# A fused attention and mixture kernel: a buffer for the third raw tile, two clears on VectorE, and a new place for six weight copies

## The chip, the cores and the metric

The kernel runs on one core of a Trainium2 chip. The metric is the device time of one execution in microseconds; of several executions the median is given. Engines: TensorE (PE, with its weight loads as PEld), VectorE (DVE), ScalarE (ACT), GpSimd (POOL) and SyncE (SP), whose queue issues nearly all loads and many of the stores.

## What is computed

Three layers follow one another on 8 batches of 576 tokens. The reference, cut to what matters:

```python
def attn(q, k, v, w_phi):                  # 8 heads of 64, d_feat 128
    def phi(x):
        proj = x @ w_phi
        proj = proj - max(abs(proj))       # over the features
        return concat([exp(proj), exp(-proj)])
    kv = einsum('bhsf,bhsd->bhfd', phi(k), v)
    z = sum(phi(k), axis=2)
    return (phi(q) @ kv) / (phi(q) @ z + 1e-06)

def moe(x):                                # 4 experts, the best 2 per token
    for e in range(4):
        a = softmax(causal(0.125 * (x @ wq[e]) @ (x @ wk[e]).T))
        out += gate[e] * (a @ (x @ wv[e]) @ wo[e])

def moe2(x):                               # mixes each token with the one before
    k = relu(xk @ w_k); v = (k * k) @ w_v
    return sigmoid(xr @ w_r) * v
```

## The kernel before, in words

The first layer is `favor`. For each batch and each half of the heads (`g` 0 and 1) the keys come as five tiles, `GROUPS`: four of 256 tokens and, third, one of 128. A key tile (`k_unit`) goes through a chain. `load` (line 273) brings the raw tile on SP's queue; `sp` splits it into a high part on ScalarE (`hi`, line 97) and a low part on POOL (`lo`, line 100), so that fp32 products come out of fp32r matmuls; `proj` makes three matmuls per 128 tokens, high by high, high by low, low by high (lines 288 to 290), into a PSUM tile `pj`, of which there are two for batch 0; `norm` reduces the maximum (line 298) and subtracts it (line 300, `pm`) on VectorE; `norm2` makes the two exponentials `ph` on ScalarE (lines 323 and 324); `kvmm` multiplies them with the values `vx`, loaded at line 315, in fp32 (line 343, `kv`). Batch 0 has ten key tiles, called one to ten here. Query tiles take a similar way over `tq` (line 370), `num` (386), `xs` (393) and `xt` (400).

The raw tiles have the tag `raw` with two buffers. The third load can be issued when tile one's high and low part have been made. `skewed` runs these stages as a software pipeline, and `weave` interleaves `favor` with the other streams: `moe1`, `compose` (the output weights times the third layer's, line 117 `fo`), `decodes` (weights that come as 64-bit floats), `load_moe1` and `gates_keys` (`rk`). From this the framework's scheduler makes one fixed order for each engine, by its own estimate of times; each engine then takes its instructions in that order.

Ahead of the weave stand the opening's pieces. The projection weights `wphi` are loaded and split on VectorE (lines 99 and 100). VectorE clears `one`, with which six filler matmuls are made on TensorE (line 138, `busy`). `clear_pads` clears padding on POOL: `k2z` (lines 149, 150), two pieces of `vsp` (152), `at1` (154), `yf` (156). Three steps of `favor` are traced, then the loads of four constants (line 979), then the weave starts. `load_moe1` loads the query, key and value projection weights of the second layer in six pieces (line 164) and splits each, the high part by ScalarE (line 97, `wqh`, `wkh`, `wvh`), the low part by VectorE (line 100, `wql`, `wkl`, `wvl`). Output weights are loaded at line 212 (`wof`) and split on VectorE (`sw`).

Of the kernel before, what the change touches and what calls it, by code (L numbers as in the profile page):

```python
# [6 lines left out]
F32 = mybir.dt.float32  # L7
F32R = mybir.dt.float32r
AF = mybir.ActivationFunctionType
# [4 lines left out]
P = 128  # L14
# [20 lines left out]
def place(fns, at):  # L35
    out = [None] * (at[-1] + 1)
    for f, a in zip(fns, at):
        out[a] = f
    return out
# [37 lines left out]
def fused_kernel(ctx: ExitStack, tc: tile.TileContext, qT, kT, vx, wphi, wq, wk, wvg, wo, mu, w64, ident, cmask, tri, out):  # L77
    nc = tc.nc
# [13 lines left out]
    def eng(c):  # L92
        return {'v': nc.vector, 'p': nc.gpsimd}[c]

    def split(hi, lo, src, eh=None, el=None):
        if eh == 'a':
            nc.scalar.activation(hi, src, AF.Copy)  # L97
        else:
            nc.vector.tensor_copy(hi, src)
        (el or nc.vector).tensor_sub(lo, src, hi.bitcast(F32))  # L100

    def evac(e, o, i):
        if e == 'a':
            nc.scalar.activation(o, i, AF.Copy)
        else:
            nc.vector.tensor_copy(o, i)
    state = {}

    def tg(n):
        return dict(tag=LATE.get(n, TAGS[n]) if 'favored' in state else TAGS[n], bufs=2)  # L110
# [19 lines left out]
    pF = phF.enter_context(tc.tile_pool(name='pF', bufs=1))  # L130
# [16 lines left out]
    def clear_pads():  # L147
        for t in K2Z:
            nc.gpsimd.memset(t[64:P, 0].bitcast(F32), 0.0)
            nc.gpsimd.memset(t[0:64, 1].bitcast(F32), 0.0)  # L150
        for t in VSP:
            nc.gpsimd.memset(t[64:P, 4].bitcast(F32), 0.0)
        for t in AT1:
            nc.gpsimd.memset(t[64:P, 1280:1600].bitcast(F32), 0.0)
        for t in YF:
            nc.gpsimd.memset(t[:, 0:1], 0.0)

    def load_moe1():
        for src, h, l, n in ((wq, wqh, wql, 'p a b c -> p (a b c)'), (wk, wkh, wkl, 'p a b c -> p (a b c)'), (wvg, wvh, wvl, 'p a b -> p (a b)')):
            hf, lf, sf = (h.rearrange(n), l.rearrange(n), src.rearrange(n))  # L160
            w = hf.shape[1] // 2
            for i in range(2):
                s_ = pA.tile([P, S], F32, name='wst1', tag='a', bufs=3)
                nc.sync.dma_start(s_[:, :w], sf[:, i * w:(i + 1) * w])
                split(hf[:, i * w:(i + 1) * w], lf[:, i * w:(i + 1) * w], s_[:, :w], 'a')
                yield 40

    def decode(pool, i, rawkw, sq, cost=1, pool_raw=None):
# [87 lines left out]
    def spans(t, h0):  # L256
        if t < 4:
            return [(0, P, h0, P * t)]
        if t > 4:
            return [(0, P, h0 + 1, P * t - S)]  # L260
        return [(0, 64, h0, 512), (64, P, h0 + 1, 0)]

    def favor(b):
        kvbank = {}

        def proj_stages(src, g, u, dst, first=False):
            tl = GROUPS[u]
            nt = len(tl)
            n = nt * P

            def load():
                t_ = pF.tile([P, 256], F32, name='raw', tag='raw', bufs=2)
                nc.sync.dma_start(t_[:, :n], src[b, g, :, tl[0] * P:tl[0] * P + n])
                dst['raw'] = t_

            def sp():
                hi = pF.tile([P, 256], F32R, name='hi', tag='hi', bufs=2)
                lo = pF.tile([P, 256], F32R, name='lo', tag='lo', bufs=2)
                split(hi[:, :n], lo[:, :n], dst['raw'][:, :n], 'a', eng('p' if b else 'p' if first else 'p'))
                dst['hl'] = (hi, lo)  # L280

            def proj():
                ps = psA.tile([P, 512], F32, name='pj', tag='f' if b else 's', bufs=2)
                hi, lo = dst['hl']
                for i in range(nt):
                    c = slice(i * P, (i + 1) * P)
                    o = ps[:, i * 256:(i + 1) * 256]
                    nc.tensor.matmul(o, hi[:, c], wph, start=True, stop=False)  # L288
                    nc.tensor.matmul(o, hi[:, c], wpl, start=False, stop=False)  # L289
                    nc.tensor.matmul(o, lo[:, c], wph, start=False, stop=True)  # L290
                dst['ps'] = ps
                return nt * 327

            def norm():
                g = 2 * nt
                ps = dst['ps'][:, :g * P].rearrange('p (g f) -> p g f', f=P)
                m = pF.tile([P, 4], F32, name='m', tag='m', bufs=3)
                nc.vector.tensor_reduce(m[:, :g], ps, axis=AX.X, op=OP.max, apply_absolute_value=True)  # L298
                pm = pF.tile([P, 512], F32, name='pm', tag='pm', bufs=3)
                nc.vector.tensor_sub(pm[:, :g * P].rearrange('p (g f) -> p g f', f=P), ps, m[:, :g].unsqueeze(2).to_broadcast([P, g, P]))  # L300
                dst['pm'] = pm
            return (load, sp, proj, norm)
        fk = [0, 2, 4, 5, 7]

        def k_unit(g, u):
            d = {}
            tl = GROUPS[u]
            nt = len(tl)
            load, sp, proj, norm = proj_stages(kT, g, u, d, True)

            def norm3():
                v_ = pF.tile([P, 2, 2, 65], F32, name='vx_', tag='vx', bufs=3)
                t0 = tl[0] + (u > 2)
                nv = 2 if u == 2 else nt
                nc.sync.dma_start(v_[:, :nv], vx[b, g, :, t0:t0 + nv])
                d['v'] = v_
                norm2()

            def norm2():
                norm()  # L320
                n = nt * 256
                kp = pF.tile([P, 2, 512], F32, name='ph', tag='ph', bufs=2)
                nc.scalar.activation(kp[:, 0, :n], d['pm'][:, :n], AF.Exp)
                nc.scalar.activation(kp[:, 1, :n], d['pm'][:, :n], AF.Exp, scale=-1.0)  # L324
                d['kp'] = kp

            def kvmm(sel):
                cost = 0
                for i, t in enumerate(tl):
                    for lo_, hi_, hp, s0 in spans(t, 2 * g):  # L330
                        if len(spans(t, 2 * g)) == 2 and hp != 2 * g + sel:
                            continue
                        new = (hp, b) not in kvbank
                        if new:
                            bank = psK.tile([P, 512], F32, name='kv', tag='kv', bufs=1)
                            kvbank[hp, b] = (bank if b == 0 else bank[:, :260]).rearrange('p (r d) -> p r d', r=4)
                        bank = kvbank[hp, b]
                        end = s0 + (hi_ - lo_) == S
                        for r in range(4):
                            c0 = (2 * i + r // 2) * P  # L340
                            v = d['v'][:, i + (lo_ > 0)]
                            v = v.rearrange('p j d -> p (j d)')[:, 2 * (r // 2):2 * (r // 2) + P] if b == 0 else v[:, r // 2]
                            nc.tensor.matmul(bank[:, r, :], d['kp'][:, r % 2, c0:c0 + P], v, start=new and r == 0, stop=end, skip_group_check=True)  # L343
                            cost += 224
                        if end:
                            kvt = pF.tile([P, 260], F32, name='kvs', tag=f'kvs{b % 2}', bufs=4)
                            if b == 0:
                                k4 = kvt.rearrange('p (r d) -> p r d', r=4)
                                evac('a', k4[:, 0:2], bank[:, 0:2, 0:65])
                                evac('a', k4[:, 2:4], bank[:, 2:4, 63:P])  # L350
                            else:
                                evac('a', kvt, bank.rearrange('p r d -> p (r d)'))
                            kvs[hp, b] = kvt
                return cost
            if nt == 1:
                return place([load, sp, proj, norm3, lambda: kvmm(0), lambda: kvmm(1)], fk + [fk[-1] + 1])
            return place([load, sp, proj, norm3, lambda: kvmm(0)], fk)
# [438 lines left out]
    def moe2():  # L796
# [173 lines left out]
        def all_():  # L970
            yield from first()
            yield from skewed([t for c in range(NC_) for t in chunk(c)])
        return all_()
    clear_pads()
    fs, ms, rk, m2 = (favors(), skewed(moe1()), skewed(gates_keys()), moe2())
    for _ in range(3):
        next(fs)
    for dst, src in ((idn, ident), (cm, cmask), (trs, tri), (mus, mu)):
        nc.sync.dma_start(dst, src)
# [55 lines left out]
```

## Time and profile before

| | |
|---|---|
| median of 3 runs | 1240.56 us (1239.51 to 1241.06) |
| the profiled execution | 1243.16 us |
| its span, first to last instruction | 1241.2 us |
| TensorE busy | 1207.8 us (97%) |
| VectorE busy | 941.5 us (76%) |
| ScalarE busy | 817.8 us (66%) |
| POOL busy | 428.1 us (34%) |
| mean granted clock of TensorE | 0.997 |

The rows come from the one profiled execution, its sums stand against 1243.16 us. Times in rows count from the span's start. A matmul's record includes the time in which it drains, so neighbouring records overlap, and the distance between starts tells the pace. The fp32 matmuls have two records each.

### The profile page before, as it was taken

How to read it: one execution, taken by the hardware profiler on the slowest of the kernel's cores; microseconds unless marked ns; L12 is line 12 of the kernel's file. 1: busy time of each engine (PE TensorE's matmuls, PEld its weight loads, DVE VectorE, ACT ScalarE, POOL GpSimd, SP SyncE). 2: the span in 40 equal slices, each digit the busy share in tenths (PEclk: the TensorE clock that was granted, in tenths of full speed). 3: DMA queues.
4: the chain of work that ended last, by engine and by line, in shares of the span. 5: the costliest groups of instructions: out<-in, count | busy, mean ns of one | idle time of the engine just before them, and what ended most of it. 6: DMA issues, size and time to landing. Idle time of an engine off the chain costs nothing.

```text
span 1241.2 us, 26673 instructions
## 1 busy us (share of the span) xinstructions
PE 1207.8 (97%) x9014; PEld 1168.1 (94%) x9014; DVE 941.5 (76%) x2493; ACT 817.8 (66%) x2008; POOL 428.1 (34%) x630
## 2 busy tenths in 40 slices
PE   8999999999999999999999999989999999999998
PEld 7899989999999999999999999988898899999998
DVE  7875988888977777887888768857757677756866
ACT  6565767667767776775668767577668575456534
POOL 5542666445643333644544533332211100000000
PEclk9999999999999999999999999999999999999999
DMA  7323125313224443454456444675788998899843
GB/s 205 93 85 90 63 84 163 110 54 104 102 91 145 137 152 116 121 168 144 124 157 181 125 139 121 183 232 164 231 277 279 311 354 288 291 309 301 283 146 128
DMA packets 159271, 212.71 MB, mean 171 GB/s; under 512 B 34464, under 2 KB 115232, under 8 KB 159136
## 3 DMA queue, kind: packets, MB, share of 16 engines
q1 hardware_dynamic: 145312, 192.12, 49.7%
q10 hardware_dynamic: 13824, 18.88, 4.2%
q8 instruction: 73, 1.20, 0.4%
q14 instruction: 62, 0.51, 0.1%
HBM read 145.94 MB, written 65.01 MB: 170 GB/s over the span
## 4 chain that ended last, share of the span: by engine, by line
PE 82%; DVE 6%; DMA 5%; ACT 2%; POOL 2%; issue 1%; SPq 0%; ACTq 0%; POOLq 0%; DVEq 0%
PE rk L117 16%; PE vacc L909 13%; PE kv L343 10%; PE num L386 8%; PE qk L117 7%; PE vp L117 4%; PE yp L601 3%; PE at L566 3%; PE pj L288 3%; PE fo L117 2%; PE pj L290 2%; PE pj L289 2%; PE tq L370 2%; PE sc L528 2%; PE sc L529 2%; DMA wt<-wf 1%
## 5 line engine op out<-in xcount | busy, mean ns | idle before, releaser
L559 POOL TENSOR_SCALAR a<-a,sv,gw 128x128 f32<-128x128 f32 (+4 forms) x160 | 107.5, 673 | 226.8 <-DVE sv L553 90.0
L100 POOL TENSOR_TENSOR lo<-raw,hi 128x256 fp32r<-128x256 f32 (+1 forms) x160 | 109.2, 685 | 183.5 <-ACT hi L97 170.2
L386 PE MATMUL num<-kvs,ph 128*128 128x65 f32 (+1 forms) x1280 | 142.0, 262 | 0.2 <-DVE xs L393 0.2
L386 PEld LDWEIGHTS num<-kvs,ph 128*128 128x128 f32 (+1 forms) x1280 | 137.1, 181 | 4.1 <-issue 1.2
L298 DVE TENSOR_REDUCE m<-pj 128x4 f32<-128x512 f32 (+1 forms) x160 | 100.7, 631 | 35.2 <-PE pj L290 33.8
L909 PE MATMUL vacc<-XT,wch 128*128 128x384 f32 x480 | 123.4, 334 | 0.7 <-DVE XT L100 0.7
L548 ACT ACTIVATE a<-sc,sv 128x128 f32<-128x128 f32 (+2 forms) x192 | 98.1, 513 | 16.9 <-DVE sv L543 9.1
L741 DVE TENSOR_TENSOR z<-rk,z 128x384 f32<-128x384 f32 x144 | 79.1, 551 | 39.6 <-PE rk L117 32.8
L300 DVE TENSOR_TENSOR pm<-pj,m 128x512 f32<-128x512 f32 (+1 forms) x160 | 100.2, 629 | 4.6 <-ACT ph L324 2.0
L543 DVE TENSOR_REDUCE sv<-sc 128x1 f32<-128x128 f32 (+2 forms) x192 | 88.5, 468 | 5.1 <-PE sc L529 1.9
L288 PE MATMUL pj<-wph,hi 128*128 128x256 f32 x288 | 90.0, 313 | 2.1 <-DVE pm L300 1.2
L97 ACT ACTIVATE XT<-kx 128x1536 fp32r<-128x1536 f32 x40 | 59.4, 1487 | 47.8 <-PE vacc L909 40.4
L100 DVE TENSOR_TENSOR XT<-kx,XT 128x1536 fp32r<-128x1536 f32 x40 | 70.1, 1753 | 24.6 <-ACT XT L97 24.5
L909 PEld LDWEIGHTS vacc<-XT,wch 128*128 128x128 f32 x480 | 86.8, 188 | 1.1 <-DVE XT L100 1.1
L97 ACT ACTIVATE hi<-raw 128x256 fp32r<-128x256 f32 (+1 forms) x160 | 62.0, 392 | 33.1 <-PE pj L289 8.8
L290 PE MATMUL pj<-wph,lo 128*128 128x256 f32 x288 | 82.5, 287 | 0.4 <-POOL lo L100 0.4
L289 PE MATMUL pj<-wpl,hi 128*128 128x256 f32 x288 | 82.0, 285 | 0.0
L909 PE MATMUL vacc<-XT,wcl 128*128 128x384 f32 x240 | 79.5, 334 | 0.0
L566 PE MATMUL at<-idn,a 128*128 128x128 f32 (+2 forms) x480 | 72.9, 261 | 5.1 <-POOL a L559 5.0
L743 ACT ACTIVATE z<-z 128x384 f32<-128x384 f32 x96 | 50.1, 521 | 33.7 <-DVE z L741 32.5
L583 DVE TENSOR_TENSOR at1l<-at,at1h 128x384 fp32r<-128x384 f32 (+3 forms) x128 | 59.2, 462 | 13.9 <-ACT at1h L582 11.5
L582 ACT ACTIVATE at1h<-at 128x384 fp32r<-128x384 f32 (+3 forms) x128 | 53.4, 418 | 24.3 <-PE at L566 16.9
(531 smaller groups left out, 3692.0 us busy)
## 6 DMA issues: line engine op xcount, KB each, us to landing
wt<-wf SPq DMA_DIRECT2D x216, 256.0 KB, 3.3
kd<-z ACTq DMA_DIRECT2D x96, 192.0 KB, 3.2
kx<-kd SPq DMA_DIRECT2D x21, 768.0 KB, 6.7
yd<-yt SPq DMA_DIRECT2D x16, 864.0 KB, 4.5
kd<-z SPq DMA_DIRECT2D x48, 192.0 KB, 3.8
zs<-kd SPq DMA_DIRECT2D x12, 768.0 KB, 6.9
out_dram<-o SPq DMA_DIRECT2D x24, 384.0 KB, 3.2
raw<-in_kT_dram SPq DMA_DIRECT2D x64, 128.0 KB, 2.4
```

Source lines behind the costliest of these rows:

```text
L97: nc.scalar.activation(hi, src, AF.Copy)
L100: (el or nc.vector).tensor_sub(lo, src, hi.bitcast(F32))
L117: nc.tensor.matmul(ps, a, m, start=first and i == 0, stop=last and i == n - 1)
L288: nc.tensor.matmul(o, hi[:, c], wph, start=True, stop=False)
L289: nc.tensor.matmul(o, hi[:, c], wpl, start=False, stop=False)
L290: nc.tensor.matmul(o, lo[:, c], wph, start=False, stop=True)
L298: nc.vector.tensor_reduce(m[:, :g], ps, axis=AX.X, op=OP.max, apply_absolute_value=True)
L343: nc.tensor.matmul(bank[:, r, :], d['kp'][:, r % 2, c0:c0 + P], v, start=new and r == 0, stop=end, skip_group_check=True)
L386: nc.tensor.matmul(ps[lo_:hi_, i, j, :], d['qp'][:, hf, c0 + lo_:c0 + hi_], kvs[hp, b][:, r * 65:(r + 1) * 65], start=hf == 0, stop=hf == 1)
L559: eng(asc).tensor_scalar(a[:m, :nk], a[:m, :nk], rc[:m], WT[b][:m, i, e:e + 1], op0=OP.mult, op1=OP.mult)
L566: nc.tensor.transpose(ps[:kw, jj * m:jj * m + m], d['a'][:m, jj * P:jj * P + kw], idn[:m, :m])
L909: nc.tensor.matmul(ps, a[:, f, dp], m[:, f], start=j in (0, 1, 5) and n == 0, stop=n == 11, skip_group_check=True)
```

## The change

It has three parts. The third raw tile of batch 0 takes its buffer from the tag `xs`, which has the same size and is first used by query tiles; four steps of `favor` are traced ahead of the constants instead of three. The two clears of `vsp` are VectorE's. And the copies of each of the six weight pieces may be issued only behind a key tile's subtraction on VectorE and its second exponential on ScalarE: piece one behind key tile two, and so on to piece six behind tile seven. That is a rule for the order on each engine, no wait at run time.

```diff
+    marks = []
+
+    @contextmanager
+    def behind(n):
+        with ExitStack() as es:
+            for ins in marks[n]:
+                es.enter_context(tc.issue_after(getattr(ins, 'ins', ins)))
+            yield
...
     def clear_pads():
...
         for t in VSP:
-            nc.gpsimd.memset(t[64:P, 4].bitcast(F32), 0.0)
+            nc.vector.memset(t[64:P, 4].bitcast(F32), 0.0)
...
     def load_moe1():
+        k = 1
...
-                split(hf[:, i * w:(i + 1) * w], lf[:, i * w:(i + 1) * w], s_[:, :w], 'a')
+                with behind(min(k, 9)):
+                    split(hf[:, i * w:(i + 1) * w], lf[:, i * w:(i + 1) * w], s_[:, :w], 'a')
+                k += 1
...
             def load():
-                t_ = pF.tile([P, 256], F32, name='raw', tag='raw', bufs=2)
+                extra = first and b == 0 and g == 0 and u == 2
+                t_ = pF.tile([P, 256], F32, name='raw', tag='xs' if extra else 'raw', bufs=1 if extra else 2)
...
             def norm():
...
-                nc.vector.tensor_sub(pm[:, :g * P].rearrange('p (g f) -> p g f', f=P), ps, m[:, :g].unsqueeze(2).to_broadcast([P, g, P]))
+                dst['sub'] = nc.vector.tensor_sub(pm[:, :g * P].rearrange('p (g f) -> p g f', f=P), ps, m[:, :g].unsqueeze(2).to_broadcast([P, g, P]))
...
             def norm2():
...
-                nc.scalar.activation(kp[:, 1, :n], d['pm'][:, :n], AF.Exp, scale=-1.0)
+                e_ = nc.scalar.activation(kp[:, 1, :n], d['pm'][:, :n], AF.Exp, scale=-1.0)
                 d['kp'] = kp
+                if b == 0:
+                    marks.append((d['sub'], e_))
...
-    for _ in range(3):
+    for _ in range(4):
         next(fs)
```

The scheduler's order moves with this. Line numbers of the changed kernel are 8 to 14 higher.

SP's queue, from the second raw tile on. `raw_167` before and `raw_163` now is tile three, `raw_173` tile four, `raw_186` tile five. Before:

```order
L273 DMA raw_157<-in_kT_dram 128x256
L979 DMA idn_60<-in_ident_dram 128x128
L979 DMA cm_61<-in_cmask_dram 128x128
L979 DMA trs_62<-in_tri_dram 128x16
L979 DMA mus_63<-in_mu_dram 128x8
L315 DMA vx__188<-in_vx_dram 128x260
L315 DMA vx__210<-in_vx_dram 128x260
L315 DMA vx__238<-in_vx_dram 128x260
L273 DMA raw_167<-in_kT_dram 128x128
L273 DMA raw_173<-in_kT_dram 128x256
L164 DMA wst1_879<-in_wq_dram 128x512
```

Now:

```order
L285 DMA raw_157<-in_kT_dram 128x256
L285 DMA raw_163<-in_kT_dram 128x128
L993 DMA idn_60<-in_ident_dram 128x128
L993 DMA cm_61<-in_cmask_dram 128x128
L993 DMA trs_62<-in_tri_dram 128x16
L993 DMA mus_63<-in_mu_dram 128x8
L285 DMA raw_173<-in_kT_dram 128x256
L285 DMA raw_186<-in_kT_dram 128x256
L327 DMA vx__188<-in_vx_dram 128x260
L327 DMA vx__210<-in_vx_dram 128x260
L327 DMA vx__238<-in_vx_dram 128x260
L173 DMA wst1_879<-in_wq_dram 128x512
```

Tile three's load stands ahead of the constants, and the loads of tiles four and five ahead of the three value tiles.

VectorE, from the reduction of tile two on (`pm_214` is tile two, `pm_242` three, `pm_272` four). Before:

```order
L298 TENSOR_REDUCE m_212<-pj_197 128x4
L298 TENSOR_REDUCE m_240<-pj_219 128x2
L300 TENSOR_TENSOR pm_214<-pj_197,m_212 128x512
L300 TENSOR_TENSOR pm_242<-pj_219,m_240 128x256
L100 TENSOR_TENSOR wql_110<-wst1_879,wqh_109 128x512
L100 TENSOR_TENSOR wql_110<-wst1_975,wqh_109 128x512
L99 CAST sw_678<-wof_680 128x512
L100 TENSOR_TENSOR sw_679<-wof_680,sw_678 128x512
L298 TENSOR_REDUCE m_270<-pj_247 128x4
L100 TENSOR_TENSOR wkl_112<-wst1_1074,wkh_111 128x512
L99 CAST sw_678<-wof_711 128x512
L300 TENSOR_TENSOR pm_272<-pj_247,m_270 128x512
```

Now:

```order
L310 TENSOR_REDUCE m_212<-pj_197 128x4
L310 TENSOR_REDUCE m_240<-pj_219 128x2
L312 TENSOR_TENSOR pm_214<-pj_197,m_212 128x512
L312 TENSOR_TENSOR pm_242<-pj_219,m_240 128x256
L100 TENSOR_TENSOR wql_110<-wst1_879,wqh_109 128x512
L310 TENSOR_REDUCE m_270<-pj_247 128x4
L99 CAST sw_678<-wof_680 128x512
L310 TENSOR_REDUCE m_299<-pj_277 128x4
L99 CAST sw_678<-wof_711 128x512
L100 TENSOR_TENSOR wql_110<-wst1_975,wqh_109 128x512
L312 TENSOR_TENSOR pm_272<-pj_247,m_270 128x512
```

The second piece of `wql` stands between the reductions of tiles four and five and the subtraction of tile four, and the first key weights' piece is gone from there. On ScalarE the two copies `wqh` stood between the exponentials of tiles one and two; now the first one follows tile two's and the second tile three's.

TensorE, near 163 us of the trace of before, where its order first differs again after the opening. Before:

```order
L117 MATMUL fo<-wth,sw 128x256
L117 MATMUL fo<-wtl,sw 128x256
L117 MATMUL fo<-wth,sw 128x256
L566 MATMUL at<-idn,a 128x128 x4
L117 MATMUL fo<-wth,sw 128x256
L117 MATMUL fo<-wtl,sw 128x256
L528 MATMUL sc<-k_2099,qs 128x128
L529 MATMUL sc<-k2z_138,qs 128x128
L117 MATMUL fo<-wth,sw 128x256
L528 MATMUL sc<-k_2099,qs 128x256
L529 MATMUL sc<-k2z_138,qs 128x256
```

Now:

```order
L580 MATMUL at<-idn,a 128x128 x4
L542 MATMUL sc<-k_2099,qs 128x128
L543 MATMUL sc<-k2z_138,qs 128x128
L542 MATMUL sc<-k_2099,qs 128x256
L543 MATMUL sc<-k2z_138,qs 128x256
L400 MATMUL num<-kvs,ph 128x65 x8
L125 MATMUL fo<-wth,sw 128x256
L300 MATMUL pj<-wph,hi 128x256
L301 MATMUL pj<-wpl,hi 128x256
L302 MATMUL pj<-wph,lo 128x256
```

The output weights' matmuls `fo` stood between the transposes `at` and the scores `sc`, and now come behind scores and `num`. From here to the end the order differs in many places. From the start of the query tiles near 47 us to this place it is the same.

## Rows read from the trace of the kernel before

**Rows 1.** The page: busy time per engine, and the chain that ended last.
```profile
PE 1207.8 (97%) x9014; PEld 1168.1 (94%) x9014; DVE 941.5 (76%) x2493; ACT 817.8 (66%) x2008; POOL 428.1 (34%) x630
...
PE 82%; DVE 6%; DMA 5%; ACT 2%; POOL 2%; issue 1%; SPq 0%; ACTq 0%; POOLq 0%; DVEq 0%
```

**Rows 2.** Windows: length; PE, PEld, DVE, ACT, POOL busy; clock; DMA share, GB/s.
```profile
0.00:14.48 14.48, 10.98 (x39) 9.34 (x40) 7.08 (x15) 6.79 (x13) 7.32 (x19) 1.00 0.72 205
14.48:47.00 32.52, 31.61 (x275) 31.22 (x275) 26.54 (x52) 21.88 (x56) 20.37 (x29) 1.00 0.55 158
47.00:162.00 115.00, 109.61 (x932) 105.40 (x932) 86.72 (x259) 73.12 (x194) 51.50 (x74) 0.99 0.27 83
162.00:1241.20 1079.20, 1055.64 (x7779) 1022.10 (x7775) 821.17 (x2169) 716.05 (x1746) 348.93 (x511) 1.00 0.57 181
```

**Rows 3.** Timeline of PE, opening: start, length, instruction [idle before it and releaser].
```profile
5.81 0.58 PE L290 MATMUL pj<-wph,lo 128*128 128x256 f32 x1 [0.37 <-POOL lo L100]
6.19 0.41 PE L288 MATMUL pj<-wph,hi 128*128 128x256 f32 x1
6.41 0.41 PE L289 MATMUL pj<-wpl,hi 128*128 128x256 f32 x1
...
8.64 0.55 PE L288 MATMUL pj<-wph,hi 128*128 128x256 f32 x1 [0.75 <-DVE pm L300]
...
10.56 3.87 PE L343 MATMUL kv<-vx__188,ph 128*128 128x128 f32 x16 [0.95 <-ACT ph L323]
...
14.45 0.30 PE L289 MATMUL pj<-wpl,hi 128*128 128x256 f32 x1
...
14.94 0.28 PE L290 MATMUL pj<-wph,lo 128*128 128x256 f32 x1
15.06 1.95 PE L343 MATMUL kv<-vx__210,ph 128*128 128x128 f32 x16
16.76 0.36 PE L288 MATMUL pj<-wph,hi 128*128 128x256 f32 x1
16.96 0.28 PE L289 MATMUL pj<-wpl,hi 128*128 128x256 f32 x1
```

**Rows 4.** Timeline of POOL, opening.
```profile
3.15 1.04 POOL L152 MEMSET vsp<- 64x512 f32 x2
4.13 0.36 POOL L154 MEMSET at1h<- 64x320 f32 x1
...
5.04 1.41 POOL L100 TENSOR_TENSOR lo<-raw,hi 128x256 fp32r<-128x256 f32 x2
```

**Rows 5.** Timeline of SP's queue, opening: when loads are issued.
```profile
4.01 0.43 SPq L315 DMA_DIRECT2D vx__188<-in_vx_dram  x1
...
5.78 1.01 SPq L273 DMA_DIRECT2D raw<-in_kT_dram  x2
```

**Rows 6.** Timeline of ACT, opening.
```profile
9.57 0.42 ACT L97 ACTIVATE hi<-raw 128x256 fp32r<-128x256 f32 x1 [1.21 <-DMA raw<-in_kT_dram]
9.89 0.61 ACT L323 ACTIVATE ph<-pm 128x512 f32<-128x512 f32 x1
```

**Rows 7.** Timeline of DVE, opening.
```profile
0.90 0.48 DVE L135 MEMSET one<- 128x512 f32 x1 [0.90 <-PEq L1023]
...
2.83 0.44 DVE L99 CAST wph<-wst 128x256 fp32r<-128x256 f32 x1 [1.31 <-DMA wst<-in_wphi_dram]
...
7.07 0.69 DVE L298 TENSOR_REDUCE m<-pj 128x4 f32<-128x512 f32 x1 [3.35 <-PE pj L290]
7.80 0.69 DVE L300 TENSOR_TENSOR pm<-pj,m 128x512 f32<-128x512 f32 x1
...
17.42 0.68 DVE L300 TENSOR_TENSOR pm<-pj,m 128x512 f32<-128x512 f32 x1
```

**Rows 8.** Windows of 10 us, columns as in rows 2.
```profile
155.00:165.00 10.00, 7.64 (x61) 7.05 (x61) 6.70 (x29) 5.79 (x16) 7.11 (x9) 0.83 0.29 105
935.00:945.00 10.00, 8.46 (x39) 7.23 (x39) 8.10 (x23) 8.45 (x22) 1.81 (x3) 0.83 0.92 322
```

**Rows 9.** Timeline of PE, near 158 us.
```profile
158.17 0.90 PE L566 MATMUL at<-idn,a 128*128 128x128 f32 x3 [2.36 <-POOL a L559]
```

More of the change, by code (lines that the diff above doesn't have):

```diff
@@ L1 @@
-from contextlib import ExitStack
+from contextlib import ExitStack, contextmanager
 import numpy as np
```

## The prediction

> **What bounds the kernel now.** I read the page first, then a table of four stretches, then the opening engine by engine. The page gives TensorE 97% of the span busy and 82% of the chain that ended last [rows 1], so time is won where TensorE stands still or runs slowly. The table puts the 33.4 us in which it stands still in place: 3.50 us before 14.48 us, 0.91 to 47, 5.39 to 162, 23.56 in the long rest [rows 2].
>
> The opening has a second loss. Successive projection matmuls of 256 columns start 0.22 us apart at first (6.19 to 6.41) and 0.12 us apart later (14.94, to the next group at 15.06) [rows 3]: 1.2 GHz first, 2.4 GHz after. The change comes between the group of 10.56 us, 16 records in 3.87 us, and the short record of 14.45 us; the next such group has its 16 in 1.95 us [rows 3]. I put it at 14.5 us. The granted-clock column shows 1.00 from the start all the same [rows 2], so in the opening the durations tell the clock. From 10.56 us to the rise the engine worked without a stop, 3.9 us; before that it had stopped for 0.37 us (for the low part from POOL), 0.75 us (for VectorE's subtraction) and 0.95 us (for the exponential) [rows 3].
>
> Followed back, these stops hang on two things. POOL's first low part starts at 5.04 us because its clears last until then [rows 4]. And the third raw tile waits for a buffer that this low part frees: its load and the fourth's are issued from 5.78 us [rows 5]. The fourth arrives at 9.57 us. ScalarE takes its instructions in order and stands before that tile while tile one is ready for its exponential: VectorE's subtraction for it starts at 7.80 and runs 0.69 us, the exponential starts at 9.89 [rows 6, 7].
>
> **The change, part by part.**
>
> *The clears.* POOL loses the two that occupy it from 3.15 us for 1.04, overlap included, or 0.98 to the next [rows 4]. Its first low part then runs from 4.06 to 4.77 us, the second to 5.47. VectorE gains two clears of 512 columns. No row shows them there; the nearest is its own clear of 512 columns on 128 partitions, 0.48 us [rows 7], the far end POOL's 0.52 each. Both lie in VectorE's 1.31 us of idling ahead of 2.83 us, where it waits for the first weights [rows 7]: it would be done by about 2.5. I cost them at nothing; with that wait gone, 0.96 us would sit on the path to the first projection.
>
> On TensorE the low-part matmul of 5.81 us had been held for 0.37 us, so the engine was free at 5.44; it can follow its predecessor one step of 0.21 after 5.03, at 5.24, and, not being a restart, takes 0.22 instead of 0.38 us to the next (5.81 to 6.19) [rows 3]. That is 0.57 + 0.16 = 0.73 us. The reduction of 7.07 and the subtraction of 7.80 [rows 7] move by as much; the latter is done at 7.76 instead of 8.49. The third projection waits for its PSUM buffer until then: it moves from 8.64 to 7.91 us and frees the engine at about 8.7.
>
> *The raw tile.* Its load goes ahead of four small constants. They are each one issue, under half a microsecond, later, and none is read by an instruction of the first 14 us. Loads four and five wait for the low parts (4.77 and 5.47) and now stand ahead of the three value tiles, whose first moves from 4.01 [rows 5] to about 6.0 us. The landing is the doubtful part: the fourth raw tile took some 3.3 us, from the second half of the pair issued at 5.78 to 9.57, when three value tiles were ahead of it [rows 5, 6]; the first weights were there at 2.83, at most 2.8 us after anything could be issued [rows 7]. With fewer loads ahead I take 2.4, and 3.3 as the far end. Value tile one is then there at 8.4 us (9.3), raw tile four at 7.3 (8.1). ScalarE splits off raw tile four's high part in 0.42 us and does the exponential of 0.61 us [rows 6] from 7.85 to 8.46.
>
> So the first keys-times-values group starts when the last of TensorE (8.7), exponential (8.46) and value tile (8.4) is ready: 8.7 us for 10.56, **1.86 us earlier**; 1.3 at the far end.
>
> *The clock.* Until the rise a microsecond is worth half. By the end of the slow stretch, half of the idle removed is won, and half of what the rise comes earlier. The engine now works without a stop from 7.9 us. If the rise follows that as it followed 10.56, it comes at 11.8 instead of 14.5: 0.93 + 1.35 = **2.3 us**. A rise that doesn't move gives 0.9. One that comes with the first projections, by 7 us, would give more than 3, but VectorE's chain (next part) lets no more than about 2.9 through. I take 2.3, because the only rise in the rows followed unbroken work.
>
> *The weights' copies.* Six on ScalarE, six subtractions on VectorE; none is added or removed. Two ScalarE copies no longer stand between exponentials one and two. On VectorE the subtraction of tile four now comes behind two reductions, two casts and one of these subtractions, at 0.69 for a reduction or subtraction and 0.44 for a cast [rows 7] 2.95 us after its own reduction begins. The sixth projection waits for it. Tile four would be projected at 12.7 us, the subtraction done near 16.3; TensorE, after the fifth projection and one and a half groups of 1.7 us (15.06 to 16.76) [rows 3], is there at 16.0. Before, that subtraction began at 17.42 [rows 7]. The wait of 0.3 us is new, and the 0.91 us of idling between 14.48 and 47 [rows 2] are there to be displaced; I count nothing for either. The copies' readers, the first query and key matmuls, come after 47 us.
>
> *The rest.* From 47 to 162 us TensorE's order is unchanged, and what was won is carried through. After that the scheduler has ordered nearly everything anew. All 7734 matmuls of the order are the same, but from there on the steps from an fp32 group to an fp32r one fall from 310 to 299. Such a step costs 0.20 us (16.76 to 16.96) instead of 0.12 [rows 3]: 11 x 0.08 = 0.9 us, times the 82% of the chain that is TensorE, **0.7 us**. The waits I take as unchanged in sum; nothing in the old trace shows the new ones.
>
> *Sum.* 2.3 + 0.7 = 3.0 us. The profiled execution took 1243.16 us (span 1241.20 and 1.96 around it); it would take 1240.2. The median of the runs lies 2.60 below it, so the prediction is 1240.56 - 3.0 = **1237.6 us**. A measurement of this kernel can tell some 0.2%, 2.5 us, from no change.
>
> **The rivals.**
>
> *The rise stays at 14.5 us.* For it: the projections and filler matmuls ahead of the first stop, at 5.44 us, had not brought a rise. Against: the one on record came out of unbroken work. Gain 0.9 + 0.7: **1238.9**. The Trainium skill, TensorE: Matmul & The Clock Gate, "What's actually happening", says that the chip's look at the engine runs freely and isn't restarted by the kernel. By that the rise moves in jumps or not at all, and differs between executions, which the one execution here can't show.
>
> *A stop in the middle goes away.* From 935 to 945 us TensorE idles 1.54 us and its clock averages 0.83, 10 x 0.17 = 1.7 us lost, 3.2 in all [rows 8]. This lies in the reordered part. If it is gone: **1234.4**.
>
> *New stops in the middle, slower.* At 158.17 us TensorE had waited 2.36 us for POOL's scaling of the probabilities [rows 9], and from 155 to 165 the clock averages 0.83, another 1.7 us [rows 8]. One such place costs 4.1 us. The order after 162 us could make more of them, where a scaling stands behind the weight decoding on POOL. It turns the sign from 3.0 + 2.5 = 5.5 us on, 23% more idling than the 23.56 us there now; two places give **1245.8**. For it: the whole stretch is reordered, and POOL takes its work in order. Against: the work is the same, and this stop lies in the part whose order stays.
>
> *VectorE eats the opening's gain.* If the output weights land late, the casts hold up the subtraction of tile four, and TensorE waits 2 us more at its sixth projection. Only the 0.7 remains: **1239.9**. VectorE was busy 26.54 of 32.52 us from 14.48 to 47 [rows 2], which speaks for it; that it idled half of the time before speaks against.
>
> **How the numbers follow.** Forecast 0.45, a rise that stays 0.17, a stop fewer 0.16, more stops 0.13, VectorE 0.09. The forecast's own range is 1236.0 to 1239.4: the opening between 0.9 and 2.9, the rest some tenths either way. Faster by more than 0.2% is below 1238.1: two thirds of the forecast, all of the fewer stops, a little of the first rival, 0.48. Slower: the more stops, 0.13. The same: 0.39. The range leaves out the more stops and the lower end of the fewer: 1233.5 to 1242.0.
>
> **What would show it.** In the new profile: VectorE's clears done before 2.83 us; POOL's first low part near 4.06; the exponential of tile one near 7.9 and the first keys-times-values matmul near 8.7; projection matmuls 0.12 us apart from about 12 us on. If the exponential still starts after 9.5, the step on the raw tile is wrong; if the value tile is waited for, its landing was. If the work of 47 us is reached 2 to 3 us sooner and the end isn't, the loss lies after 162 us, and TensorE's idle time there must be above 23.56 us.

## The result, and the profile after

The changed kernel takes **1258.7 us** (median of 4 executions, 1257.23 to 1260.96), the kernel before 1240.81 on the same chip: ratio 1.0134, 95% interval 1.0109 to 1.016. The forecast was 1237.6 with a range up to 1242.0, so it is wrong in sign and by 21 us. Run again beside the experiments it took 1257.09 (6 executions), ratio 1.0121 [1.0099, 1.0143].

The page of the profiled execution (span 1259.1 us), against [rows 1]: busy time of each engine, and the chain that ended last.

```profile
PE 1216.5 (97%) x9014; PEld 1174.1 (93%) x9014; DVE 937.7 (74%) x2495; ACT 817.1 (65%) x2008; POOL 426.0 (34%) x628
...
PE 79%; DVE 8%; DMA 5%; ACT 3%; POOL 2%; issue 2%; SPq 1%; ACTq 0%; POOLq 0%; DVEq 0%
```

TensorE has 3 points less of the chain, VectorE 2 more. The same four stretches as in [rows 2] (length; PE, PEld, DVE, ACT, POOL busy; granted clock; DMA share, GB/s):

```profile
0.00:14.48 14.48, 11.87 (x72) 10.88 (x73) 7.34 (x16) 7.63 (x15) 7.17 (x18) 1.00 0.71 203
14.48:47.00 32.52, 29.85 (x249) 29.45 (x248) 25.88 (x54) 20.91 (x54) 19.10 (x26) 0.95 0.54 159
47.00:162.00 115.00, 108.20 (x898) 104.08 (x896) 84.69 (x256) 71.50 (x189) 49.68 (x72) 0.97 0.25 76
162.00:1259.10 1097.10, 1066.63 (x7799) 1029.72 (x7799) 819.82 (x2173) 717.07 (x1751) 350.08 (x516) 0.99 0.56 179
```

In the first stretch TensorE now stands still 2.61 us for 3.50. Everything behind it is worse: 2.67 for 0.91 us, 6.80 for 5.39, and in the rest 1097.10 - 1066.63 = **30.5 us for 23.56**, with lower clocks in three of the four.

The opening, PE's timeline (start, length, instruction, [idle before it and what ended that]), to be read beside [rows 3]:

```profile
5.11 0.41 PE L302 MATMUL pj<-wph,lo 128*128 128x256 f32 x1
...
6.58 0.28 PE L302 MATMUL pj<-wph,lo 128*128 128x256 f32 x1
7.76 0.35 PE L300 MATMUL pj<-wph,hi 128*128 128x256 f32 x1 [0.90 <-DVE pm L312]
...
8.63 2.05 PE L357 MATMUL kv<-vx__188,ph 128*128 128x128 f32 x16 [0.28 <-DMA vx__188<-in_vx_dram]
...
11.96 1.95 PE L357 MATMUL kv<-vx__210,ph 128*128 128x128 f32 x16
13.74 1.06 PE L357 MATMUL kv<-vx__238,ph 128*128 128x128 f32 x8
17.27 0.55 PE L300 MATMUL pj<-wph,hi 128*128 128x256 f32 x1 [2.47 <-DVE pm L312]
17.62 0.42 PE L301 MATMUL pj<-wpl,hi 128*128 128x256 f32 x1
```

The low part of 5.11 is no longer held, the first keys-times-values group starts at 8.63 us, and the second at 11.96 where [rows 3] has 15.06: 3.1 us won by then. At 17.27 most of it goes: TensorE has stood still for 2.47 us, and the next projections are 0.21 us apart again (17.62 to 17.83), half speed. POOL's and ScalarE's rows of the opening, for [rows 4] and [rows 6]:

```profile
4.11 1.42 POOL L100 TENSOR_TENSOR lo<-raw,hi 128x256 fp32r<-128x256 f32 x2
```

```profile
7.03 0.42 ACT L97 ACTIVATE hi<-raw 128x256 fp32r<-128x256 f32 x1 [0.68 <-DMA raw<-in_kT_dram]
7.65 0.63 ACT L335 ACTIVATE ph<-pm 128x512 f32<-128x512 f32 x1 [0.21 <-DVE pm L312]
```

VectorE's, for [rows 7]:

```profile
1.55 1.03 DVE L160 MEMSET vsp<- 64x512 f32 x2 [0.16 <-issue]
...
12.36 0.68 DVE L310 TENSOR_REDUCE m<-pj 128x4 f32<-128x512 f32 x1
14.09 0.90 DVE L99 CAST sw<-wof 128x512 fp32r<-128x512 f32 x1 [1.04 <-DMA wof<-in_wo_dram]
14.91 0.68 DVE L310 TENSOR_REDUCE m<-pj 128x4 f32<-128x512 f32 x1
15.51 0.41 DVE L99 CAST sw<-wof 128x512 fp32r<-128x512 f32 x1
15.85 0.68 DVE L100 TENSOR_TENSOR wql<-wst,wqh 128x512 fp32r<-128x512 f32 x1
16.45 0.68 DVE L312 TENSOR_TENSOR pm<-pj,m 128x512 f32<-128x512 f32 x1
```

The subtraction that TensorE waits for begins at 16.45 us. Its own reduction was done at 13.04; between them VectorE stands 1.04 us before a cast whose output weights have not landed. At the first numerator matmul TensorE is still 0.9 us ahead (40.19 for 41.07). The loss comes behind that. Windows of after (columns as before) in which the clock drops, for [rows 8], and the place of [rows 9]:

```profile
47.00:81.00 34.00, 30.41 (x244) 28.34 (x243) 22.24 (x67) 17.48 (x45) 12.35 (x19) 0.90 0.22 67
159.00:169.00 10.00, 7.63 (x61) 6.94 (x61) 6.85 (x28) 6.07 (x18) 5.90 (x8) 0.83 0.29 105
820.00:830.00 10.00, 7.81 (x46) 7.39 (x45) 4.77 (x12) 7.36 (x20) 4.70 (x5) 0.83 0.81 251
957.00:967.00 10.00, 8.03 (x38) 7.14 (x37) 6.37 (x18) 8.22 (x21) 1.83 (x3) 0.83 0.92 325
```

```profile
162.06 0.55 PE L580 MATMUL at<-idn,a 128*128 128x128 f32 x3 [2.37 <-POOL a L573]
```

The stop of 2.36 us near 158 us stands as it was, 3.9 us later. Matching the matmuls of both traces one by one gives how far after lags: -0.9 us at 40, 3.9 from 81 to 150, 9.2 at 400, 11.7 at 800, 20.0 at 1000, 17.4 at 1200. Where the order differs, single matmuls lie several microseconds to either side of these medians. So 4.8 us are lost between 40 and 81 us, 3.4 of them by the clock (0.90 over the 34 us from 47), and some 14 in the reordered rest.

### The profile page after: what moved, and what is told of

The parts are those of the page before. It is cut to its first block, busy times and chain, and to the rows that moved or that the text cites. A ratio compares the mean times of both kernels' runs of the same rounds, so it can differ in the third digit from the quotient of the medians.

```text
span 1259.1 us, 26725 instructions
## 1 busy us (share of the span) xinstructions
PE 1216.5 (97%) x9014; PEld 1174.1 (93%) x9014; DVE 937.7 (74%) x2495; ACT 817.1 (65%) x2008; POOL 426.0 (34%) x628
## 4 chain that ended last, share of the span: by engine, by line
PE 79%; DVE 8%; DMA 5%; ACT 3%; POOL 2%; issue 2%; SPq 1%; ACTq 0%; POOLq 0%; DVEq 0%
PE rk L125 15%; PE vacc L923 12%; PE kv L357 10%; PE num L400 8%; PE qk L125 7%; PE vp L125 4%; PE at L580 3%; PE yp L615 3%; PE pj L300 3%; PE pj L302 2%; PE pj L301 2%; PE fo L125 2%; PE tq L384 2%; PE sc L542 2%; PE sc L543 2%
## 5 line engine op out<-in xcount | busy, mean ns | idle before, releaser
L400 PE MATMUL num<-kvs,ph 128*128 128x65 f32 (+1 forms) x1280 | 144.9, 266 | 0.2 <-DVE xs L407 0.2
L400 PEld LDWEIGHTS num<-kvs,ph 128*128 128x128 f32 (+1 forms) x1280 | 139.8, 184 | 5.0 <-issue 1.6
L755 DVE TENSOR_TENSOR z<-rk,z 128x384 f32<-128x384 f32 x144 | 79.4, 551 | 37.5 <-PE rk L125 28.7
```

The lines of the kernel that those rows point to most:

```text
L400: nc.tensor.matmul(ps[lo_:hi_, i, j, :], d['qp'][:, hf, c0 + lo_:c0 + hi_], kvs[hp, b][:, r * 65:(r + 1) * 65], start=hf == 0, stop=hf == 1)
```

## The experiments

Two theories. **One: order.** The loss comes from the new order in which the scheduler puts the rest of the program, not from what the three parts do. **Two: parts.** Something in the parts themselves costs (the shared buffer of the third tile, the queued copies).

To tell them apart, some kernels hold a given order: a table of instruction numbers, and an edge that orders each instruction behind the one ahead of it on its engine. Waits, buffers and instructions stay. Holding an order costs nothing that shows: the changed kernel, held in its own order with a single exchange, took 1256.85 us, and 1257.09 without the table (both below).

```
+    for e, text in ORDER.items():
+        steps = np.frombuffer(zlib.decompress(base64.b85decode(text)), np.int16)
+        ins = [by[e][k] for k in np.cumsum(steps.astype(int))]
+        for a, b in zip(ins, ins[1:]):
+            tc.add_manual_dep(b, a.name, edge, reason='order')
```

The order tables of the next two join one program's order up to about 66 us to the other's from there.

**The change up to 66 us, the old order behind it.** Source: the changed kernel and `follow`.

> The changed kernel, with its own order on every engine up to about 66 us and from there the order of the kernel before, held by order edges. Theory 1 (the loss lies in the new order of the rest): 1244 to 1246 us, the 3.8 us that the changed kernel is behind at its projections of 81 us and nothing more. Theory 2 (the opening's stop and slow clock push the whole pipeline out of step): 1254 us or more.

Measured 1247.24 us, ratio 1.0035 [1.0009, 1.0061].

**The old kernel up to 66 us, the new order behind it.** Source: the kernel before and `follow`.

> The kernel before, with its own order up to about 66 us and from there the order of the changed kernel. Theory 1: 1253 to 1256 us, the whole loss of 18 less the 3.8 us of the first part. Theory 2: 1240 to 1243 us.

Measured 1253.0 us, ratio 1.0082 [1.0059, 1.0105]. The rest of each, first the change's parts in the old order, then the old parts in the new order:

```profile
162.00:1242.00 1080.00, 1056.27 (x7792) 1022.40 (x7791) 821.17 (x2170) 717.87 (x1750) 351.53 (x513) 1.00 0.57 181
```

```profile
162.00:1251.70 1089.70, 1060.98 (x7768) 1025.69 (x7767) 818.64 (x2168) 714.57 (x1742) 346.72 (x512) 0.99 0.56 179
```

TensorE stands still 23.7 us in the old order and 28.7 in the new one. The old kernel with nothing but another order of its rest loses some 10 us (1253.0 for 1242.1 on that chip); the change in the old order keeps 4 to 5, 1.2 more than the upper end that theory one had for it. So theory one holds for the larger part, and 4 to 5 us are left that go with the parts or with the order up to 66 us. The first row is of an execution of 1243.78 us, 3.5 below that kernel's median: what its other executions lose, the row doesn't show.

**One part alone, three times.** The order is the scheduler's own in each.

```
-            nc.gpsimd.memset(t[64:P, 4].bitcast(F32), 0.0)
+            nc.vector.memset(t[64:P, 4].bitcast(F32), 0.0)
```

> The kernel before with the two clears on VectorE alone, ordered by the scheduler. It has a third order of the rest, different from both. Theory 1: any time from 1238 to 1260 us, with the difference after 162 us; a value far from 1240.8 shows that an order like this alone costs as much. Theory 2: 1239 to 1241 us, since the opening gains at most 0.7 us.

```
-    for _ in range(3):
+    for _ in range(4):
...
+                extra = first and b == 0 and g == 0 and u == 2
+                t_ = pF.tile([P, 256], F32, name='raw', tag='xs' if extra else 'raw', bufs=1 if extra else 2)
```

> The kernel before with the third raw tile's own buffer and the fourth step of favor alone, ordered by the scheduler. Its order after 162 us is within some rows that of the changed kernel. Theory 1: 1252 to 1258 us. Theory 2: with the weights' copies in their old place the subtraction of tile four comes sooner, the stop of 2.47 us is shorter, and the time is 1238 to 1246 us.

```
+                with behind(min(k, 9)):
+                    split(hf[:, i * w:(i + 1) * w], lf[:, i * w:(i + 1) * w], s_[:, :w], 'a')
+                k += 1
```

> The third part alone: only the weight copies are queued behind key tiles two to seven. The scheduler then leaves the order from about 50 us as in the kernel before. Theory 1: within 0.2% of the kernel before, 1240 to 1244 us on this chip. Theory 2 (the queued copies are what costs): 1246 us or more.

Measured: clears 1245.53, ratio 1.0019 [0.9995, 1.0043]; buffer 1256.56, 1.0104 [1.0071, 1.0136]; copies 1241.61, 0.9993 [0.9976, 1.001]. With the copies alone the order of the rest stays the old one; the buffer alone gives nearly the order of the change; the clears alone give a third. The same third order comes out for both of these parts without the copies:

> The third raw tile's buffer and the clears on VectorE, without the queued weight copies, everything in the order that the scheduler gives by itself. That order of the rest is nearly the one of the run with the clears alone (1245.5 us), not that of the buffer alone (1256.6) nor of the change. Theory 1 (the time follows the order that comes out, not the parts): 1241 to 1246 us. Theory 2 (the third tile's buffer is what costs): 1253 us or more.

Measured 1242.82, ratio 1.0013 [0.9999, 1.0027]. The buffer, alone 14 us above the kernel before on its chip, is 1 above where the clears go with it. So most of the time follows the order that comes out, and not the edit. Within each class the traces have TensorE's instructions in one and the same sequence from 70 us on (the last column is from the profiled executions):

| order of the rest | kernels | median us | PE still after 162 us |
|---|---|---|---|
| old | before; copies alone; the joined ones | 1241 to 1247 | 21.7 to 23.7 |
| third | clears alone; buffer and clears | 1242.8, 1245.5 | 23.0 |
| new | the change; buffer alone; old parts in the new order | 1253 to 1259 | 28.7 to 32.7 |

The old order and the third overlap; the new one stands apart.

**Where the order costs, and what the 4 us are.** One kernel has the new order up to 500 us only, one the change's parts and new order up to the first numerator at 40 us only, one the same cut without the queued copies.

> The changed kernel with its own order on every engine up to about 500 us, from there the order of the kernel before. Theory 1a (the loss of the rest is many small stops spread over the whole rest): about half of it is kept, 1250 to 1254 us. Theory 1b (it sits in the few large stops after 800 us, at the weight combination of 820 us, at 960 and at 1020 to 1035 us): 1246 to 1249 us, next to the 1247 of the run cut at 66 us.

> The changed kernel with all three of its parts, but every engine keeps the new order only up to the first numerator matmul (about 40 us) and then has the order of the kernel before; the run with the same idea cut at 66 us took 1247.2 us. Theory 1 (the loss is a matter of order, and the 4 us which that run lost lie in VectorE's new order between 47 and 66 us): 1240 to 1243 us, at the place of 81 us level with the kernel before or up to 1 us ahead. Theory 2 (the three parts cost something in themselves that shows only later, whatever the order): 1246 us or more.

> The third raw tile's buffer and the clears on VectorE, without the queued weight copies; the own order of that up to the first numerator matmul (about 40 us), from there the order of the kernel before. Theory 1: the opening's gain is carried to the end and nothing else changes, 1238 to 1241 us, 1 to 3 us below the kernel before on the same chip. Theory 2: 1246 us or more, as the buffer alone took 1256.6.

Measured 1249.55, ratio 1.0052 [1.0034, 1.007]; 1245.86, 1.0029 [1.001, 1.0048]; 1241.01, 0.9986 [0.997, 1.0001]. The first lags by 1.2 us at 150, 6.7 at 400 and no more to 800: about 5 us of the new order's price lie between 162 and 400, and the other 8 or so behind 500, as the lags of after say too. So it is spread, as theory 1a had it; the time itself lies between the ranges of 1a and 1b. The second missed the first theory's range and came out just under the second's: the 4 us don't lie in the order between 47 and 66 alone. The third is the best of them; its interval just reaches 1.

**Mending the opening.** In that third kernel TensorE still waits 2.34 us at the same projection as in the change, without the queue:

```profile
18.08 0.36 PE L289 MATMUL pj<-wph,hi 128*128 128x256 f32 x1 [2.34 <-DVE pm L301]
```

VectorE now does reductions and subtractions of key tiles first.

```
 VectorE, 12 to 25 us (the number is the key tile's)
-wql wql m4 sw wkl m5 sw pm4 sw pm5 sw wkl da m6 wvl dc m7 pm6 wvl da pm7 dr
+wql m4 pm4 wql m5 pm5 sw sw wkl sw sw wkl da m6 pm6 wvl dc m7 pm7 wvl da dr
```

> The run of the two parts with the old order from 40 us (1241.0 us), and on VectorE between 12 and 25 us the reductions and subtractions of key tiles ahead of the low parts and casts of weights that stood before them; nothing else moves. Theory 1 (the opening's gain is lost at the sixth projection, where TensorE waits 2.34 us for a subtraction that stands behind weights on VectorE): that stop falls below 0.5 us, TensorE is 2 us ahead of the kernel before at 40 us, 1238 to 1240 us. Theory 2 (VectorE has too much to do there, whatever goes first: the stop comes a little later instead): 1240.5 to 1242 us, level with the run without it.

Measured 1244.79, ratio 1.0016 [0.9999, 1.0033], above the ranges of both theories. The stop did what the second one named. Its PE row:

```profile
18.25 1.50 PE L344 MATMUL kv<-vx__238,ph 128*128 128x128 f32 x7 [2.17 <-ACT kvs L104]
```

The projections run without the wait, and TensorE stands still as long at the next group, for an eviction on ScalarE that is behind weights still on their way. The opening is bound by several engines at once near 18 us. Up to 250 us this execution (1245.64 us) is level with the one without the mending; then it loses 5 us at half speed from 269 us on (last section), and the two executions end 4.5 us apart. Whether its other executions lost theirs there, no trace shows.

**Mending stops of the new order.** The change again, and the change with one pair on ScalarE exchanged.

```
 ScalarE, near 823 us
-wch<-wst
 at1h<-at
+wch<-wst
```

> The changed kernel itself once more, so that it stands beside the next run on the same chip. Both theories: 1256 to 1260 us. Its stop of 2.19 us before the transposes near 825 us should be there again.

> The changed kernel with its own order on every engine but for one pair on ScalarE near 823 us: the eviction at1h of the transposed probabilities now goes ahead of a copy of a combination weight (wch), behind which it stood while that copy waited for its load. Theory 1 (each stop of the new order is a small piece of work that stands behind another on an engine that takes its instructions in order): the stop of 2.19 us near 825 us shrinks to 0.5 or less, and the time falls by 1.7 us, by up to 3.4 where the 3.4 us at half speed behind it go too; the rest stays, 1253 to 1257 us. Theory 2 (TensorE is late for another reason there, or the next wait takes its place): within 0.5 us of the changed kernel beside it.

Measured 1257.09 (above) and 1256.85, the latter 1.0114 [1.0093, 1.0136]. The change's stop, PE's timeline, and ScalarE's:

```profile
823.67 0.48 PE L580 MATMUL at<-idn,a 64*128 64x64 f32 x5 [1.72 <-POOL wcl L100]
```

```profile
821.68 0.63 ACT L97 ACTIVATE wch<-wst 128x512 fp32r<-128x512 f32 x1 [1.38 <-DMA wst<-wc]
822.22 0.58 ACT L596 ACTIVATE at1h<-at 128x512 fp32r<-128x512 f32 x1
```

With the exchange, PE:

```profile
823.28 0.51 PE L580 MATMUL at<-idn,a 64*128 64x64 f32 x5 [0.26 <-POOL a L573]
```

The releaser named is POOL's `wcl`; but that wait is for two semaphores, and the eviction behind ScalarE's waiting copy is what had held it, for the stop of 1.72 us shrinks to 0.26 when it goes first. The medians can't tell a gain of 2 us here. So four places at once:

```
 ScalarE 823 us:  at1h ahead of wch          VectorE 345 us: pm ahead of dr
 ScalarE 1024 us: z<-rk ahead of zs          VectorE 682 us: pm, sv ahead of dc
```

> The changed kernel with its own order but for four places, where the instruction that TensorE waits for goes ahead of one that it stood behind: on ScalarE the eviction at1h ahead of a weight copy (near 823 us) and the eviction of rk ahead of the table load and zs (near 1024), on VectorE the subtraction pm ahead of a decoding step dr (near 345), and pm and a score reduction ahead of a decoding step dc (near 682). By the stops of the two profiles of the change: about 1.8 + 0.9 + 0.7 + 1.0 = 4.4 us, and up to 3.4 more where half-speed stretches go with them. Theory 1 (the loss is the sum of such stops): 1249 to 1254 us, ratio to before near 1.008. Theory 2 (a stop mended turns into the next wait): 1255 us or more, ratio 1.011 or above as with one exchange.

Measured 1257.57, ratio 1.0119 [1.0102, 1.0136]: **nothing won**. Stops of 0.74, 1.71, 1.72 and 1.94 us in the change's second profile, 6.1 in all, became these:

```profile
346.33 0.54 PE L125 MATMUL qk<-XT,wqh 128*128 128x288 f32 x2 [0.40 <-DVE yf L624]
...
681.43 0.63 PE L384 MATMUL tq<-idn,pm 128*128 128x128 f32 x4 [0.44 <-DVE pm L312]
682.48 1.33 PE L125 MATMUL rk<-yc__9714,wt 128*128 128x384 f32 x6 [0.42 <-DVE z L755]
...
1032.53 1.01 PE L923 MATMUL vacc<-XT,wch 128*128 128x384 f32 x2 [2.63 <-ACT u L104]
```

A mended stop comes back within microseconds as a few shorter ones, or as one further on. Part of what was won may have gone to the clock: its mean over the profiled execution is 0.990, over the change's second one 0.993. The largest stop of the old order, near 157 us, was mended in the best joined kernel to see how that goes:

```
 VectorE: reciprocal of the row sums right behind their addition (153.9 instead of 156.0 us)
 POOL:    a<-a,sv,gw ahead of wo<-cb,wo
```

> The two parts with the old order from 40 us (1241.0 us, ratio 0.9986) and one exchange at the stop of 2.36 us near 157 us, which the kernel before has too: on VectorE the reciprocal of the row sums goes right behind their addition, on POOL the scaling of the probabilities ahead of the low part of the output weights. Theory 1 (a stop costs its length and mostly the 3.4 us at half speed behind it): the stop shrinks to 0.7 us or less, 1.7 to 3.4 us are won, 1237 to 1239.5 us, ratio 0.996 to 0.9975. Theory 2 (the next wait takes its place): 1240.5 to 1242, ratio 0.998 or above.

Measured 1241.7, ratio 0.9992 [0.9978, 1.0007]: again the next wait takes its place. Without the mending, PE's timeline, and the windows behind the stop:

```profile
157.21 0.55 PE L567 MATMUL at<-idn,a 128*128 128x128 f32 x3 [2.35 <-POOL a L560]
...
160.29 1.28 PE L387 MATMUL num<-kvs,ph 128*64 128x65 f32 x16
...
173.06 0.39 PE L567 MATMUL at<-idn,a 128*128 128x128 f32 x2
```

```profile
157.00:164.00 7.00, 6.79 (x53) 6.27 (x54) 3.70 (x14) 4.88 (x13) 5.58 (x8) 0.76 0.36 123
164.00:172.00 8.00, 8.00 (x70) 7.80 (x70) 7.87 (x29) 5.54 (x19) 4.18 (x7) 1.00 0.18 50
```

With it:

```profile
154.94 0.55 PE L567 MATMUL at<-idn,a 128*128 128x128 f32 x3 [0.36 <-POOL a L560]
...
157.28 0.97 PE L387 MATMUL num<-kvs,ph 128*64 128x65 f32 x16
...
159.80 0.39 PE L117 MATMUL fo<-wtl,sw 128*128 128x256 f32 x1 [0.43 <-POOL wtl L100]
...
172.38 0.44 PE L567 MATMUL at<-idn,a 128*128 128x128 f32 x2 [0.27 <-POOL a L560]
```

```profile
157.00:164.00 7.00, 6.20 (x56) 5.29 (x56) 4.42 (x16) 4.75 (x13) 4.80 (x7) 1.00 0.34 113
164.00:172.00 8.00, 7.81 (x61) 6.97 (x60) 7.87 (x31) 6.19 (x21) 4.83 (x8) 1.00 0.19 52
```

Stop and half-speed stretch are gone, the numerators start 3.0 us sooner, and 12 us later only 0.7 are left, of which 0.3 had been there ahead of the stop. VectorE is busy 7.87 of 8 us in both: TensorE, ahead, waits for it and for POOL in small pieces. What stands as TensorE's loss there is shared with VectorE.

No kernel was below the one before by more than the measurement tells; the two parts in the old order from 40 us came nearest.

## Why the prediction was wrong, point by point

- **The clears**: right. POOL's first low part runs at 4.11 us (4.06 forecast), VectorE's clears are done at 2.58, ahead of the weights' cast at 2.85, and the low part of 5.11 isn't held.
- **The raw tile**: right. The exponential of tile one starts at 7.65 (7.85), the first keys-times-values group at 8.63 (8.7), held a last 0.28 us by its value tile, which was named as the doubtful part. That 8.7 fits so well is in part luck: it was the time at which TensorE would be free, and by the prediction's own rows that is 8.88 (7.91, then 0.35, 0.21 and the last record's 0.41). TensorE was free at 8.35, because the clock had risen, and the value tile came last.
- **The clock**: wrong in its time and its cause. The second group comes 3.1 us sooner (2.3 forecast), since the rise came by 6.6 us and not at 11.8: the case that the prediction named and set aside. It doesn't follow unbroken work alone: with the old opening one execution had it at 14.5 us and another by 6 (last section).
- **The weights' copies**: mis-sized, and the rival *VectorE eats the opening's gain* was right. Forecast 0.3 us, measured 2.47: TensorE was there at 14.8 instead of 16.0, and the subtraction was done at 17.1 instead of 16.3, not least because output weights that had not landed held VectorE for 1.04 us. The half-speed stretch behind the stop was in no term. The wait isn't the queue's doing: without the queue it is 2.34.
- **The rest**: **the step that failed**, at "The waits I take as unchanged in sum". They went from 23.56 to 30.5 us, 7 of the 14 lost there, and with the old parts in the new order to 28.7. Half-speed stretches are about half of the other 7: a window of 10 us at 0.83 loses 1.7, and such stretches stand at 163, 826, 863 and 962 us. The first is the one of [rows 8] near 158 us, moved behind 162, and the old rest had one near 940; so two are new, 3.4 us. With the buffer alone the same order has 32.7 us of waits and, besides the one moved, a single such stretch: the waits are the steadier part. What the last 3 to 4 us are isn't shown. The gain of 0.7 us from fewer fp32-to-fp32r steps can't be told from nothing: adding up, over all neighbouring matmuls, the median step that their two forms take in the old trace gives 0.9 us less for the new order where forms are told apart by the tiles written and read (1188.1 and 1187.2), and 1.4 more by the tile written and the shapes (1175.5 and 1176.9). And "carried through" failed from 47 to 162: TensorE's order is the same there, VectorE's isn't, and the lead of 0.9 us became a lag of 3.9, most of it the half-speed stretch before 81 us. That stretch doesn't follow from the order alone: the second profile of the change has it too, but two joined kernels with the same order up to 66 us (the old order behind it, and the new one up to 500 us) have none there in their profiles, and lag 1.9 and 1.2 us at 81.
- *New stops in the middle* was the mechanism, with a chance of 0.13 and 1245.8 us for two stops of 4.1. There are many short ones instead: the profile of before has 9 stops over 0.6 us after the first 20 us, that of after 18. Their number isn't the price either: the third order has 15, and TensorE stands still 23.0 us there, less than before.

What stays open: which property of the new order costs. It isn't a few stops that can be mended one by one. Nor is it settled why the change's parts up to 40 us keep 4 us in the old order, where the same without the queue keeps none. The profiles of the two kernels that have the change's opening in the old order don't show this loss: these executions took 1243.78 and 1240.91 us, 3.5 and 5.0 below their medians, and end 0.8 us behind and 2.2 us ahead of the profile of before. Executions of both with a granted clock under 0.995 took longer than the others (medians 1249.1 against 1243.9, and 1247.7 against 1243.2), so half-speed stretches are a part of it; where they stand, no trace shows.

## What to carry to other kernels

Where a scheduler orders the whole program, a small edit at its start can draw another order of everything behind it, and that is the larger part of what is measured: orders of the same rest lay some 10 us apart, and the buffer that cost 14 us alone cost 1 together with the clears, where another order came out. Hold the old order behind the place of the edit before crediting or blaming it. Compare medians of many executions: two of the profiles here were 3.5 and 5 us faster than their kernel's median. And where a second engine is busy nearly all the time, a stop of the first one isn't a price: mend it in one run before counting it.

## What the runs showed of the hardware

**The clock's rise does not come from the opening alone.** The kernel with the old opening (old parts to 66 us), PE's timeline:

```profile
5.81 0.39 PE L290 MATMUL pj<-wph,lo 128*128 128x256 f32 x1 [0.54 <-POOL lo L100]
6.04 0.28 PE L288 MATMUL pj<-wph,hi 128*128 128x256 f32 x1
6.15 0.28 PE L289 MATMUL pj<-wpl,hi 128*128 128x256 f32 x1
...
9.71 3.88 PE L343 MATMUL kv<-vx__188,ph 128*128 128x128 f32 x16 [0.24 <-ACT ph L323]
```

Its projections are 0.11 us apart at 6 us, where [rows 3] has 0.22, and the group of 9.71 takes 3.88 us again, at half speed: the clock had risen and fallen. The Trainium skill, TensorE: Matmul & The Clock Gate, "What's actually happening", says that the look at the engine runs freely and isn't reset when a kernel starts; these two executions of one opening agree. The same stop also meets the clock differently: a stop of 1.18 us at 269 us was followed by half speed in the run with the mended opening (granted clock 0.63 from 269 to 283 us) and by none in its neighbour without the mending (1.00). So one profile doesn't give a stop's price.

**VectorE and POOL hold each other up.** In the change's second profile, VectorE's timeline, then POOL's:

```profile
680.33 1.59 DVE L196 SCALAR_TENSOR_TENSOR dc<-hz,da 128x256 int32<-128x256 int32 x1
```

```profile
680.21 1.43 POOL L100 TENSOR_TENSOR yt<-dl,yt 128x576 fp32r<-128x576 f32 x1
```

In the first profile:

```profile
682.29 0.41 DVE L196 SCALAR_TENSOR_TENSOR dc<-hz,da 128x256 int32<-128x256 int32 x1
```

```profile
682.18 1.83 POOL L100 TENSOR_TENSOR yt<-dl,yt 128x576 fp32r<-128x576 f32 x1
```

Either one is long, depending on the execution, and the stop behind it was 1.71 us in one and 0.53 in the other. The Trainium skill, SBUF — State Buffer, "SBUF: two separate sides", says that a VectorE instruction with two inputs in SBUF and a POOL one that reads SBUF share one pair of ports, which the first takes whole for an instruction while the other blocks. The rows agree: POOL's row is 0.40 us longer where VectorE's takes 0.41, and VectorE's is 1.18 us longer and ends 0.28 us behind POOL's where POOL's takes 1.43.
